# A 64-byte gap ahead of GT's tile and a 40-column offset inside wk's slot, in a gated mix of a long convolution and linear attention

## The chip, the core and the metric

The kernel runs on one core of one Trainium2 chip. The metric is the device time of one execution in microseconds (us), lower is better; 1 us is 1000 ns. TensorE (PE) does the matmuls and, beside them, loads the weights of the next one (PEld); DVE is VectorE, ACT is ScalarE, POOL is GpSimd, SP issues the DMAs.

## What is computed

Input x has 2048 rows of 640 columns. The result mixes two branches with a gate per row:

```python
g = _sigmoid((x * gate_w).sum(-1, keepdims=True))
a = _A_ref(x, ...)       # per column: convolution with a kernel of length 2048, plus x * Dskip
b = _B_ref(x, wqkv, wo)  # linear attention: 32 heads of 20 columns
return g * a + (1 - g) * b
# in _B_ref: phi(t) = where(t > 0, t + 1, exp(t)) + 1e-6
#   kv = sum_s phi(k)_s v_s ; z = sum_s phi(k)_s
#   o  = phi(q) kv / (phi(q) z + 1e-6) ; b = o @ wo
```

## The kernel before

Every fp32 matrix is held as two float32r tiles, a high part `h` (a rounded copy) and a low part `l` (the rest), and a product is three matmuls, all accumulated in one PSUM bank. This is `mm3` (line 104): high by high, low by high, high by low. In a matmul one operand is loaded into the array beforehand (128 columns, the stationary one, PEld's `LDWEIGHTS`), the other streams past it (the moving one, up to 512 columns). `pe.matmul(out, a, b)` has `a` stationary and `b` moving. In rows of the profile, `fp<-pTh,Mh` names the moving tile first and the stationary one second.

The work has three stretches.

1. **Start, to about 36 us.** The first four row tiles of x and the weights wk arrive by DMA, are split into high and low, and the key products of those four tiles are computed as the pieces land (`k_first`, line 441; matmuls at L449).
2. **The loop over T = 1 to 15 (line 530), to about 147 us.** Each round computes, for the 128 rows of tile T, the keys in two halves: `k_mm(T, 0)` (line 183) multiplies by `wkA`, 320 columns of wk and two copies of the gate's column, so 322 moving columns, 15 matmuls; `k_mm(T, 1)` multiplies by `wkB`, 320 moving columns, 15 matmuls. Around these stand the matmuls of tile T-1 that sum phi(k) against x: `g_main` (L224, L225, L227; 512 moving columns) in the blocks 0, then 1 and 2, then 3 and 4, and `g_rest` (L238 to L240; 320 moving columns). The order of one round on TensorE from T = 4 on is k_mm by wkA (15), g block 0 (3), g blocks 1 and 2 (6), k_mm by wkB (15), g_rest (6), g blocks 3 and 4 (6). Meanwhile ACT and DVE apply phi and split the next tiles, DVE runs the scan of the convolution, and SP moves x, wv and the convolution's y.
3. **The plan (line 63, run from line 728), to the end.** `q_block` (line 630) computes a 128 by 512 tile of the queries in 15 matmuls of 512 columns, with a slice of wq stationary and x transposed moving; there are 20 of them. `kv_mm` and `m_mm` fold kv and wo into a 640 by 640 matrix M, which goes to DRAM and comes back in two tiles, `Mh` and `Ml` (`m_load`, line 692). `final_mm` (line 705) computes a 128 by 512 tile of the output in 15 matmuls with a slice of M stationary and `pqT` (phi of q, normed) moving; there are 20, the last one in two halves of 256 columns. DVE adds y to each and SP stores it.

Tiles of the pool `pc` stand in SBUF one behind the other in the order in which the program names their tags, at a fixed place for the whole run. A tag is a slot, and later tiles of the same tag take it over: slot `m1` holds GT and later Mh, `m2` holds Wv and later Ml, `wAh` and `wAl` hold `wkA` and later `wqA` (the first three of wq's five column blocks), `wBh` and `wBl` hold `wkB` and later `wqB`. The slot of `wA` has rows of 384 columns, since wqA needs them; wkA uses 322 of these. The pools `pk`, `pw` and `pq` (x, phi(k), y, the raw weights and others) come behind `pc`. The pool `px`, with x transposed (`xTh`, `xTl`) and later `pTh`, `pTl` in the same slots, stands ahead of it.

Of the kernel before, what the change touches and what calls it, by code (L numbers as in the profile page):

```python
# [39 lines left out]
P = 128  # L40
# [7 lines left out]
CA, CB = 320, 320  # L48
# [9 lines left out]
NK = sum(map(len, CONV_K.values()))  # L58
WQ = 3, 4, 0, 1, 2
QI = DH // NB  # L60


PLAN = """
# [10 lines left out]
def f32(ap):  # L74
    return ap.bitcast(F32)


def body(tc, i, outT):
    nc = tc.nc
    pe, act, dve, pool, sp = nc.tensor, nc.scalar, nc.vector, nc.gpsimd, nc.sync  # L80
# [17 lines left out]
    def hi(dst, src):  # L98
        act.activation(dst, src, AF.Copy)  # L99
# [9 lines left out]
    def col(tag, n=NB, dt=F32):  # L109
        return pc.tile([P, n], dt, tag=tag, name=tag)  # L110

    def w_tiles(n, tag, name):
        return tuple(pc.tile([P, NB, n], F32R, tag=tag + x, name=name + x) for x in "hl")
# [30 lines left out]
    zc, zs, ch = col("zc"), col("zs", 1), col("ch", 1)  # L144
    zsh, zsl = col("zsh", 2, F32R), col("zsl", 2, F32R)
    bm, zh = col("bm", P, F32R), col("zh", H)
    GT = pc.tile([P, NB, D], F32, tag="m1", name="GT")
    Wv = pc.tile([P, NB, D], F32, tag="m2", name="Wv")
    M_d = [dram.tile([D, D], F32, name=f"M_d{x}") for x in "hl"]
# [55 lines left out]
    def k_split(t):  # L205
# [4 lines left out]
        dve.scalar_tensor_tensor(l, e, EPS, f32(h), op0=OP.add, op1=OP.subtract)  # L210
        za = zacc.rearrange("p (b h i) -> p b h i", h=H, i=QI)
        dve.tensor_tensor(za, za, e.rearrange("p (h b i) -> p b h i", b=NB, i=QI), op=OP.add)
        ks[t] = (h, l)
# [28 lines left out]
    def g_out(b, eng):  # L242
        src = gps.pop(b)
        (hi if eng is act else dve.tensor_copy)(GT[:, b, :512], src)

# [4 lines left out]
    def parts(gi):  # L250
        c0, n = GRP[gi]
        return [(r, c0 + o, min(HC, n - o)) for r, o in ((0, 0), (64, HC)) if o < n]
# [13 lines left out]
    def kv_mm(pr):  # L266
        p = pqp.tile([P, 512], F32, tag="f", bufs=3, name="kvps")
        kvT = kvs[pr] = kvz[pr % 2]
        for k, gi in enumerate((2 * pr, 2 * pr + 1)):
            for b in range(NB):  # L270
                for r, c, n in parts(gi):
                    pe.matmul(p[r : r + n, k * 64 : k * 64 + n], Wv[:, b, c : c + n], GT[:, b, c : c + n],
                              start=(b == 0), stop=(b == NB - 1))
# [175 lines left out]
                pe.matmul(kp[t, hf][:, :n], (xTl if ps == 1 else xTh)[0][:, b, sl], w[ps // 2][:, b, :n],  # L449
                          start=b + ps == 0, stop=b == NB - 1 and ps == 2)  # L450

    wkA = w_tiles(3 * P, "wA", "wkA")
    wkB = w_tiles(CB, "wB", "wkB")
    raw = {}

# [59 lines left out]
    def wq_views(w, c, b0, b1):  # L515
        src = raw[c][:, :D].rearrange("p (h b i) -> p b h i", b=NB, i=QI)[:, b0:b1]
        return [src] + [v[:, c, : (b1 - b0) * P].rearrange("p (b h i) -> p b h i", h=H, i=QI) for v in w]

# [11 lines left out]
    for T in range(1, NT):  # L530
# [45 lines left out]
        if T == 2:  # L576
            act.activation(dtc, dtc, AF.Exp)
            dve.tensor_reduce(zh, ident.rearrange("p (h i) -> p h i", i=QI), axis=AX.X, op=OP.add)
            dve.tensor_copy(bm.rearrange("p (h i) -> p h i", i=QI), zh[:, :, None].to_broadcast([P, H, QI]))
        for b in CONV_P.get(T - 1, ()):  # L580
# [39 lines left out]
    def rem_out():  # L620
        for b0, b1 in ((0, 4), (4, NB)):
            tp = mbank("tp")
            for b in range(b0, b1):
                pe.transpose(tp[:, (b - b0) * P : (b - b0 + 1) * P], rem[:, b * P : b * P + P], ident)
            hi(GT[:, b0:b1, 512:], tp[:, : (b1 - b0) * P].rearrange("p (b s) -> p b s", s=P))

# [314 lines left out]
```

## Time and profile before

| | |
|---|---|
| median of 3 runs | 303.79 us (303.33 to 304.34) |
| profiled execution, its time | 304.36 us |
| profiled execution, its span | 302.6 us |
| granted TensorE clock | 0.999 |
| PE busy | 296.6 us, 98% of the span, 1627 matmuls |
| PEld busy | 255.7 us, 85% |
| DVE busy | 230.0 us, 76% |
| ACT busy | 118.8 us, 39% |
| POOL busy | 46.9 us, 15% |

The span runs from the first instruction to the last; the execution's time has 1.8 us around it. In the rows of the timeline the first number is the start in us and the second the length of the row. The lengths of matmuls overlap: one begins long before the one ahead of it is written out. What a matmul costs is therefore the distance from its start to the start of the next, which I call its spacing, and not its length.

### The profile page before, as it was taken

How to read it: one execution, taken by the hardware profiler on the slowest of the kernel's cores; microseconds unless marked ns; L12 is line 12 of the kernel's file. 1: busy time of each engine (PE TensorE's matmuls, PEld its weight loads, DVE VectorE, ACT ScalarE, POOL GpSimd, SP SyncE). 2: the span in 40 equal slices, each digit the busy share in tenths (PEclk: the TensorE clock that was granted, in tenths of full speed). 3: DMA queues.
4: the chain of work that ended last, by engine and by line, in shares of the span. 5: the costliest groups of instructions: out<-in, count | busy, mean ns of one | idle time of the engine just before them, and what ended most of it. 6: DMA issues, size and time to landing. Idle time of an engine off the chain costs nothing.

```text
span 302.6 us, 4538 instructions
## 1 busy us (share of the span) xinstructions
PE 296.6 (98%) x1627; PEld 255.7 (85%) x1627; DVE 230.0 (76%) x356; ACT 118.8 (39%) x249; POOL 46.9 (15%) x50
## 2 busy tenths in 40 slices
PE   8999999999999999999999999999999999999994
PEld 8998899999999999998887767888888888788884
DVE  2859976899899799946636779859684767788992
ACT  4465143453444435317343563651423234303200
POOL 3605240000000000000000000003133211242531
PEclk9999999999999999999999999999999999999999
DMA  6827275167868756290344553790415022244323
GB/s 190 302 88 220 77 233 185 36 192 203 256 150 252 225 181 203 80 281 14 100 147 137 205 176 110 259 341 9 114 59 186 25 77 62 69 141 172 122 92 109
DMA packets 28410, 46.00 MB, mean 152 GB/s; under 512 B 3772, under 2 KB 10828, under 8 KB 28384
## 3 DMA queue, kind: packets, MB, share of 16 engines
q1 hardware_dynamic: 28383, 45.66, 48.2%
q8 instruction: 15, 0.25, 0.4%
q14 instruction: 12, 0.09, 0.1%
HBM read 32.92 MB, written 12.72 MB: 151 GB/s over the span
## 4 chain that ended last, share of the span: by engine, by line
PE 87%; DVE 6%; DMA 3%; issue 1%; ACT 1%; SPq 1%; POOL 0%; DVEq 0%; ACTq 0%; POOLq 0%
PE fp L105 8%; PE fp L107 8%; PE fp L106 8%; PE qp L105 6%; PE qp L107 6%; PE qp L106 6%; PE k L107 6%; PE k L106 6%; PE k L105 6%; PE g L227 5%; PE g L224 5%; PE g L225 5%; PE g L449 4%; DMA M_dl<-Mgl 2%; PE r L240 1%; PE r L239 1%
## 5 line engine op out<-in xcount | busy, mean ns | idle before, releaser
L434 POOL TENSOR_TENSOR yb<-yb,gb 128x512 f32<-128x512 f32 x20 | 29.5, 1482 | 220.5 <-DMA yb<-y_d 199.2
L105 PE MATMUL fp<-pTh,Mh 128*128 128x512 f32 (+1 forms) x105 | 40.1, 382 | 0.6 <-DVE o L720 0.6
L107 PE MATMUL fp<-pTl,Mh 128*128 128x512 f32 (+1 forms) x105 | 40.2, 383 | 0.0
L106 PE MATMUL fp<-pTh,Ml 128*128 128x512 f32 (+1 forms) x105 | 40.0, 381 | 0.0
L645 DVE SCALAR_TENSOR_TENSOR qe<-qe,qr 128x512 f32<-128x512 f32 x20 | 14.1, 704 | 23.8 <-ACT qr L642 23.8
L224 PE MATMUL g<-ph,xh 128*128 128x512 f32 x80 | 31.6, 395 | 0.0
L225 PE MATMUL g<-ph,xl 128*128 128x512 f32 x80 | 31.5, 394 | 0.0
L199 ACT ACTIVATE e<-k 128x320 f32<-128x320 f32 x25 | 11.0, 439 | 51.3 <-PE k L107 51.3
L99 ACT ACTIVATE pTh<-qe 128x512 fp32r<-128x512 f32 x20 | 12.6, 633 | 40.5 <-DVE qe L681 40.4
L203 DVE SCALAR_TENSOR_TENSOR e<-e,r 128x320 f32<-128x320 f32 x32 | 16.0, 504 | 14.0 <-ACT r L200 13.9
L227 PE MATMUL g<-pl,xh 128*128 128x512 f32 x80 | 26.4, 395 | 0.1
L105 PE MATMUL qp<-xTh,wqAh 128*128 128x512 f32 x60 | 24.0, 401 | 0.0
L641 ACT ACTIVATE qe<-qp 128x512 f32<-128x512 f32 x20 | 12.0, 598 | 30.6 <-PE qp L107 26.6
L105 PEld LDWEIGHTS fp<-pTh,Mh 128*128 128x128 f32 x105 | 19.7, 188 | 5.0 <-DVE o L720 1.0
L107 PE MATMUL qp<-xTl,wqAh 128*128 128x512 f32 x60 | 23.7, 394 | 0.0
L106 PE MATMUL qp<-xTh,wqAl 128*128 128x512 f32 x60 | 23.6, 393 | 0.0
L106 PEld LDWEIGHTS fp<-pTh,Ml 128*128 128x128 f32 x105 | 19.7, 188 | 4.1
L107 PEld LDWEIGHTS fp<-pTl,Mh 128*128 128x128 f32 x105 | 19.8, 188 | 3.9
L414 DVE TENSOR_TENSOR_SCAN y<-y,cY,zero 128x512 f32<-128x512 f32 x16 | 20.5, 1278 | 0.8 <-ACT y L413 0.8
L102 DVE TENSOR_TENSOR pTl<-qe,pTh 128x512 fp32r<-128x512 f32 x20 | 15.1, 763 | 6.8 <-ACT pTh L99 6.3
L107 PE MATMUL k<-wkAl,xTh 128*128 128x322 f32 x60 | 19.0, 317 | 0.0
L106 PE MATMUL k<-wkAh,xTl 128*128 128x322 f32 x60 | 18.9, 315 | 0.0
(168 smaller groups left out, 718.2 us busy)
## 6 DMA issues: line engine op xcount, KB each, us to landing
xraw<-in_x SPq DMA_DIRECT2D x16, 320.0 KB, 5.0
u<-in_xT SPq DMA_DIRECT2D x20, 256.0 KB, 5.3
out_T<-o SPq DMA_DIRECT2D x19, 256.0 KB, 2.5
y_d<-y SPq DMA_DIRECT2D x16, 256.0 KB, 2.2
yb<-y_d SPq DMA_DIRECT2D x16, 256.0 KB, 3.1
xTraw<-in_xTt SPq DMA_DIRECT2D x12, 320.0 KB, 4.5
Wv<-in_wv SPq DMA_DIRECT2D x5, 320.0 KB, 6.8
Mh<-M_dh SPq DMA_DIRECT2D x5, 320.0 KB, 4.6
```

Source lines behind the costliest of these rows:

```text
L99: act.activation(dst, src, AF.Copy)
L102: (eng or dve).tensor_tensor(dst, src, f32(h), op=OP.subtract)
L105: pe.matmul(out, ah, bh, start=start, stop=False)
L106: pe.matmul(out, al, bh, start=False, stop=False)
L107: pe.matmul(out, ah, bl, start=False, stop=stop)
L203: dve.scalar_tensor_tensor(e, e, 1.0, r[:, :n], op0=OP.min, op1=OP.add)
L224: pe.matmul(gps[b], xh[:, s], h[:, :512], start=t == 0, stop=False)
L225: pe.matmul(gps[b], xl[:, s], h[:, :512], start=False, stop=False)
L227: pe.matmul(gps[b], xh[:, b * P : b * P + P], l[:, :512], start=False, stop=t == NT - 1)
L414: dve.tensor_tensor_scan(y, y, zero.to_broadcast([P, 512]), cY[:, c], op0=OP.add, op1=OP.add)
L434: pool.tensor_tensor(ys[j], ys[j], gbs[j // NB], op=OP.mult)
L645: dve.scalar_tensor_tensor(e, e, 1.0, r, op0=OP.min, op1=OP.add)
```

## The change

Two edits. A tile `gap` of 16 fp32 columns, 64 bytes in each partition, is named just ahead of GT and set to zero on POOL. And `wkA` becomes a view into its slot that begins at column 40 of each row of 384, so that its 322 columns stand in columns 40 to 361; writers and readers go through the same view.

```diff
+WKO = 40
...
     bm, zh = col("bm", P, F32R), col("zh", H)
+    gap = col("gap", 16)
+    pool.memset(gap, 0.0)
     GT = pc.tile([P, NB, D], F32, tag="m1", name="GT")
...
-    wkA = w_tiles(3 * P, "wA", "wkA")
+    wkA = tuple(v[:, :, WKO : WKO + CA + 2] for v in w_tiles(3 * P, "wA", "wkA"))
```

No instruction is moved on PE, DVE, ACT or SP, and none changes its shape or its waits. POOL has one more. These are its rows at the start, up to the first piece of wk's low part, before:

```order
L121 MEMSET ones 128x128
L132 MEMSET zacc 128x640
L135 MEMSET cY 128x5
L135 MEMSET zero 128x1
L141 MEMSET kvT_100 128x128
L141 MEMSET kvT_101 128x128
L102 ISA
L102 TENSOR_TENSOR wkAl<-wraw,wkAh 128x322 x5
```

And the same place now, where the lines have moved by 1 to 3:

```order
L122 MEMSET ones 128x128
L133 MEMSET zacc 128x640
L136 MEMSET cY 128x5
L136 MEMSET zero 128x1
L142 MEMSET kvT_100 128x128
L142 MEMSET kvT_101 128x128
L149 MEMSET gap 128x16
L103 ISA
L103 TENSOR_TENSOR wkAl<-wraw,wkAh 128x322 x5
```

One memset stands ahead of the first `wkAl`. Everything else that changes is where tiles lie. The table gives, from the layout of the two programs, the place of each matmul's operands within their partition, as the remainder of the byte address by 512. The slices of a stationary operand step by 512 bytes, rows of the transposed x and of pT by 2048, of M by 2560, of wkA and wqA by 1536, of wkB and wqB by 1280 (so these alternate between two remainders). The last two columns are moving minus stationary.

| matmuls | stationary, before -> after | moving, before -> after | difference before | after |
|---|---|---|---|---|
| `fp` (final_mm) | M: 64 -> 128 | pT: 128 | +64 | 0 |
| `qp`, blocks 0 to 2 | wqA: 64 -> 128 | xT: 128 | +64 | 0 |
| `qp`, blocks 3 and 4 | wqB: 64, 320 -> 128, 384 | xT: 128 | +64, -192 | 0, 256 |
| `k` by wkA | xT: 128 | wkA: 64 -> 288 | -64 | +160 |
| `k` by wkB | xT: 128 | wkB: 64, 320 -> 128, 384 | -64, +192 | 0, 256 |
| `g` (g_main) | x: 320 -> 384 | phi(k): 320 -> 384 | 0 | 0 |
| `r` (g_rest) | phi(k): 320 -> 384 | x: 320, 64 -> 384, 128 | 0, 256 | 0, 256 |

## The prediction

> **What bounds the kernel now.** I read the page's busy times and chain first, then the busy times by stretch, then the timeline of PE in pieces of half a microsecond. The page says what sets the end:
>
> ```profile
> PE 296.6 (98%) x1627; PEld 255.7 (85%) x1627; DVE 230.0 (76%) x356; ACT 118.8 (39%) x249; POOL 46.9 (15%) x50
> PE 87%; DVE 6%; DMA 3%; issue 1%; ACT 1%; SPq 1%; POOL 0%; DVEq 0%; ACTq 0%; POOLq 0%
> ```
>
> PE is busy for 98% of the span, and 87% of the chain that ended last is PE. In the busy times by stretch (start and end, length, then PE, PEld, DVE, ACT and POOL) PE has no hole in the loop or in the first part of the plan:
>
> ```profile
> 36.00:142.00 106.00, 106.00 (x615) 98.04 (x614) 88.38 (x148) 46.60 (x107) 3.71 (x6) 1.00 0.60 180
> 182.00:235.00 53.00, 53.00 (x229) 42.90 (x228) 39.71 (x53) 20.76 (x37) 9.88 (x7) 1.00 0.49 157
> 264.00:299.00 35.00, 34.58 (x165) 28.82 (x165) 30.05 (x33) 6.53 (x11) 13.79 (x9) 1.00 0.38 130
> ```
>
> The granted clock is 1.00 in all three. DVE, the next engine, has 88.38 of 106.00 us, 39.71 of 53.00 and 30.05 of 35.00: it could follow a PE that is faster by one or two per cent. So the change is worth what it does to the spacing of matmuls, nothing else. A busy PE is not an even one. Two pieces of the plan run the same shape at different spacings:
>
> ```profile
> 203.50 0.40 PE L105 MATMUL fp<-pTh,Mh 128*128 128x512 f32 x1
> 203.73 0.40 PE L106 MATMUL fp<-pTh,Ml 128*128 128x512 f32 x1
> ...
> 235.00 0.39 PE L666 MATMUL dp<-acch,bm 128*128 128x512 f32 x1
> 238.90 0.39 PE L105 MATMUL qp<-xTh,wqAh 128*128 128x512 f32 x1
> 239.14 0.39 PE L106 MATMUL qp<-xTh,wqAl 128*128 128x512 f32 x1
> 239.36 0.39 PE L107 MATMUL qp<-xTl,wqAh 128*128 128x512 f32 x1
> 239.59 0.39 PE L105 MATMUL qp<-xTh,wqAh 128*128 128x512 f32 x1
> ...
> 256.07 0.39 PE L105 MATMUL fp<-pTh,Mh 128*128 128x512 f32 x1
> ```
>
> From 203.50 to 235.00 stand nine tiles, fp and qp in turn, of 15 matmuls: 31.50 us, 3.50 a tile, 233.3 ns a matmul. From 238.90 to 256.07 stand five tiles: 17.17 us, 3.434 a tile, 228.9 ns. The work, the clock and the operands' places are the same in both; two rhythms exist, and which one holds depends on how the stretch was entered. A third, shorter one stands in the g matmuls at the end of the loop:
>
> ```profile
> 143.01 0.39 PE L225 MATMUL g<-ph,xl 128*128 128x512 f32 x1
> 143.23 0.39 PE L224 MATMUL g<-ph,xh 128*128 128x512 f32 x1
> 143.46 0.39 PE L225 MATMUL g<-ph,xl 128*128 128x512 f32 x1
> 143.69 0.84 PE L227 MATMUL g<-pl,xh 128*128 128x512 f32 x3
> 144.37 0.30 PE L238 MATMUL r<-xh,ph 128*128 128x320 f32 x1
> ```
>
> Six matmuls of 512 columns in 1.36 us, 226.7 ns each: the shortest steady spacing of this width that I find, so I call it the floor. The keys by wkA, 322 columns, have two rhythms as well. These are the first of the 15 matmuls, and the first matmul behind them, in rounds T = 4, 5, 6 and 15, and where T = 7 begins:
>
> ```profile
> 36.09 0.31 PE L105 MATMUL k<-wkAh,xTh 128*128 128x322 f32 x1
> 38.30 0.40 PE L224 MATMUL g<-ph,xh 128*128 128x512 f32 x1
> 44.81 0.31 PE L105 MATMUL k<-wkAh,xTh 128*128 128x322 f32 x1
> 47.02 0.40 PE L224 MATMUL g<-ph,xh 128*128 128x512 f32 x1
> ...
> 53.77 0.31 PE L105 MATMUL k<-wkAh,xTh 128*128 128x322 f32 x1
> 56.06 0.40 PE L224 MATMUL g<-ph,xh 128*128 128x512 f32 x1
> 56.78 0.40 PE L224 MATMUL g<-ph,xh 128*128 128x512 f32 x1
> 62.63 0.31 PE L105 MATMUL k<-wkAh,xTh 128*128 128x322 f32 x1
> ...
> 133.45 0.31 PE L105 MATMUL k<-wkAh,xTh 128*128 128x322 f32 x1
> 135.74 0.40 PE L224 MATMUL g<-ph,xh 128*128 128x512 f32 x1
> ```
>
> In T = 4 the block takes 2.21 us (147 ns a matmul), in T = 6 2.29 us (153 ns); the round takes 8.72 and 8.86 us. T = 5 (44.81 to 47.02) goes like the first; T = 15 (133.45 to 135.74) goes like the second, as do the ones between. The weight loads by form, first for 36 to 51 us, then for 54 to 142 us, show who is held up (count, busy us, mean ns):
>
> ```profile
> L106 PEld LDWEIGHTS k<-wkAh,xTl 128*128 128x128 f32 x10 | 1.9, 188 | 0.1
> L106 PEld LDWEIGHTS k<-wkAh,xTl 128*128 128x128 f32 x50 | 9.6, 192 | 0.4
> ```
>
> A load beside the slow wkA stream takes 192 ns, beside the quick one 188. The two rhythms of each width differ by 6.6 and 6.7 ns. Per column, a matmul costs (226.7 - 147) / (512 - 322) = 0.42 ns, so this step is the time of 16 columns, or 64 bytes of one partition. That is my reading of the trace: the moving stream and the weight load of the next matmul meet in SBUF, one gives way by one step of 64 bytes, and whether they meet depends on their places and on the phase.
>
> **The change part by part.** The memset of `gap`. Nearest rows, POOL's timeline:
>
> ```profile
> 1.53 0.35 POOL L141 MEMSET kvT<- 128x128 f32 x2
> 4.27 0.99 POOL L102 TENSOR_TENSOR wkAl<-wraw,wkAh 128x322 fp32r<-128x322 f32 x1 [2.39 <-DVE wkAh L487]
> ```
>
> Two memsets of 128 columns took 0.35 us together, so one of 16 costs between nothing and 0.2 us, and POOL then idles 2.39 us until DVE has cast wkAh. Cost 0; without that cover it would be up to 0.2 us ahead of the first key matmuls. The writers of wkA (DVE's cast, POOL's subtraction) write the same shape with the same row step: 0.
>
> M and wq. The stationary start moves from 64 to 128 modulo 512, and the moving one stays at 128, so the difference becomes 0 (wqB: 0 or 256). That is the difference that g has now, and r has 0 and 256. The g matmuls are the nearest rows: same width, same alternation of a high and a low stationary, long enough at 143 us to be steady, and there they stand at 226.7 ns. I take the floor for M and wq. The counts, from the groups of PE by form, and behind them two rows of the timeline:
>
> ```profile
> L105 PE MATMUL fp<-pTh,Mh 128*128 128x512 f32 x95 | 37.4, 393 | 0.6 <-DVE o L720 0.6
> L105 PE MATMUL qp<-xTh,wqAh 128*128 128x512 f32 x60 | 24.0, 401 | 0.0
> L105 PE MATMUL qp<-xTh,wqBh 128*128 128x512 f32 x40 | 15.8, 395 | 0.0
> ...
> 176.33 0.40 PE L105 MATMUL qp<-xTh,wqAh 128*128 128x512 f32 x1
> ...
> 179.60 0.39 PE L107 MATMUL qp<-xTl,wqAh 128*128 128x512 f32 x1
> ```
>
> 95 + 60 + 40 = 195 groups of three, five to a tile: 39 tiles. At the floor a tile takes 15 x 0.2267 = 3.40 us. Ten tiles run at 3.50 now (the nine above, and one whose first and last start, 14 spacings apart, are 176.33 and 179.60), the other 29 near 3.434. Saving: 10 x 0.10 + 29 x 0.034 = 1.0 + 1.0 = 2.0 us. Bounds: the shorter end is 2.0; at the longer end all 39 go to 3.50, which costs 29 x 0.066 = 1.9 us. I take 2.0 saved since g is the nearest row.
>
> wkA. The difference goes from -64 to +160, half a step of 64 bytes off: no matmul in this trace has such a difference. The nearest rows are its own two rhythms. If T = 6 to 15 run like T = 4, ten blocks save 0.08 each, 0.8 us; if T = 4 and 5 run like the rest, 2 x 0.08 = 0.2 us is lost; one more step on all 180 matmuls would cost 180 x 6.7 ns = 1.2 us. I take 0.8 saved: a stationary and a moving stream half a step apart have the least cause to fall into the meeting at -64, which took hold only after two of twelve rounds.
>
> wkB, g, r. wkB goes from -64 and 192 to 0 and 256, the differences of r; both widths are 320 columns. The rows for r:
>
> ```profile
> 51.51 0.31 PE L238 MATMUL r<-xh,ph 128*128 128x320 f32 x1
> ...
> 52.38 0.39 PE L224 MATMUL g<-ph,xh 128*128 128x512 f32 x1
> 49.31 0.31 PE L105 MATMUL k<-wkBh,xTh 128*128 128x320 f32 x1
> ```
>
> Six r matmuls take 0.87 us (145 ns), 15 by wkB from 49.31 to 51.51 take 2.20 us (147 ns): the same within rounding, cost 0. The g and r operands move together. But g behind a slow wkA block is slow too: the three from 56.06 to 56.78 us stand 0.24 us apart. Round T = 6 is 0.14 us longer than T = 4, and the wkA block explains 0.08; the other 0.06 over ten rounds is 0.6 us, which I keep for the range.
>
> Sum against the profiled execution: 304.36 - 2.0 - 0.8 = 301.6 us. This execution lies 0.6 us above the median, so 303.79 - 2.8 = **301.0 us** on the scale of the median.
>
> The Trainium skill (SBUF — State Buffer, section "Who interferes with whom") gives PE two independent read ports, one for the moving operand and one for the weight load, and says that PE never waits on anyone. By that rule the shift would save nothing, and the sum would stay at 303.8 us. The rows above speak against it: one shape at 147 and 153 ns with a load of 188 and 192 ns. No run here yet shows places alone doing it.
>
> **The rivals.**
>
> *Nothing moves (0.25).* The rhythm is set by how a stretch is entered, whatever the places: 203 and 239 us show both rhythms at the same places. Then the sum is 303.8 us, or 303.0 with wkA's 0.8 alone. A measurement of this kernel tells about 0.3%, 0.9 us, from no change, so both fall under the same. Against it: in this trace 226.7 ns stands over six matmuls only where the difference is 0.
>
> *M and wq gain, wkA stays (0.20).* 303.8 - 2.0 = 301.8 us.
>
> *Slower (0.20).* With stationary and moving tiles at the same place modulo 512, load and stream meet every time, and the long rhythm, now in 10 tiles of 39, takes all of them: 29 x 0.066 = 1.9 us, 305.7 us; with wkA one step worse 306.9. For it: the g matmuls at 56.06 us have the difference 0 and stand at 240 ns. Against it: they come right behind a slow block, and the longer run at 143 us came down to the floor. It decides from the point at which more than about half of the tiles, 29 x 0.066 / 2 = 1 us, lock in the long rhythm.
>
> **How the numbers follow.** Forecast 0.35, M and wq alone 0.20, nothing 0.25, slower 0.20. Faster by over 0.3%: 0.55; within: 0.25; slower: 0.20. The likeliest case alone spans 300.2 (with the 0.6 of g and 0.2 of scatter) to 301.8. For 8 in 10 the range takes in the second and third case and part of the slower one, whose price holds only if all tiles lock: 300.2 to 305.2 us.
>
> **What would show it.** Right: tiles of fp and qp 3.40 us long, with starts 0.227 apart, through 182 to 296 us; rounds of the loop near 8.72 us from T = 6 on; wkA's loads at 188 ns; PE still 98% busy. Half right: 3.40 with rounds still at 8.86. Wrong: tiles at 3.43 and 3.50 in other places than now (entry decides, not place), or 3.50 throughout. If PE's spacing falls and the time does not, PE will show idle time behind DVE at L720, where one wait of 0.6 us stands now.

## The result and the profile after

| | before | changed |
|---|---|---|
| median of 6 runs | 304.06 us (303.33 to 305.27) | 301.80 us (301.31 to 302.20) |
| ratio to before, 95% interval | | 0.9913 [0.9898, 0.9928] |
| span of the profiled execution | 302.6 us | 300.0 us |

The changed kernel is faster: by the ratio 0.87%, which is 2.6 us of 304.06, by the two medians 2.3 us. (Before was measured again beside it, so its median has moved from 303.79.) The profiled execution of the changed kernel took 301.86 us. Its page, busy times and chain:

```profile
PE 294.0 (98%) x1627; PEld 255.3 (85%) x1627; DVE 230.7 (77%) x356; ACT 118.4 (39%) x249; POOL 46.5 (15%) x51
PE 89%; DVE 5%; issue 1%; ACT 1%; DMA 1%; SPq 1%; POOL 0%; DVEq 0%; ACTq 0%; POOLq 0%
```

PE is busy 2.6 us less over the same 1627 matmuls, and still 98% of a span that is 2.6 us shorter. Lines are now 1 to 3 higher, so L105 to L107 of `mm3` are L106 to L108. The timeline of the stretch of nine fp and qp tiles that took 31.50 us:

```profile
202.07 0.39 PE L106 MATMUL fp<-pTh,Mh 128*128 128x512 f32 x1
...
205.50 0.39 PE L106 MATMUL qp<-xTh,wqBh 128*128 128x512 f32 x1
...
232.70 0.40 PE L669 MATMUL dp<-acch,bm 128*128 128x512 f32 x1
```

The first tile takes 3.43 us, since the way in from dp still costs something; the eight behind it take 27.20 us, 3.40 each, 226.7 ns a matmul. That is the floor named in the prediction, and the long stretches of tiles from 184 us on all come down to it. Tiles between other work, most of them before 184 us, do not: they take 3.49 to 3.59. Round T = 6 of the loop, the block by wkA and the start of round 7:

```profile
54.05 0.31 PE L106 MATMUL k<-wkAh,xTh 128*128 128x322 f32 x1
56.27 0.39 PE L227 MATMUL g<-ph,xh 128*128 128x512 f32 x1
62.78 0.31 PE L106 MATMUL k<-wkAh,xTh 128*128 128x322 f32 x1
```

2.21 us for the block (2.29 before; the rows, rounded, give 2.22) and 8.73 for the round (8.86). The weight loads of that stretch, 54 to 142 us:

```profile
L107 PEld LDWEIGHTS k<-wkAh,xTl 128*128 128x128 f32 x50 | 9.4, 188 | 0.4
```

They last 188 ns, no longer 192. The new memset on POOL, and what follows it:

```profile
1.81 0.11 POOL L149 MEMSET gap<- 128x16 f32 x1
4.40 0.98 POOL L103 TENSOR_TENSOR wkAl<-wraw,wkAh 128x322 fp32r<-128x322 f32 x1 [2.48 <-DVE wkAh L490]
```

0.11 us, and POOL still idles 2.48 us behind it. One place became slower, the last tile with its two halves of 256 columns. Before, from the timeline:

```profile
295.49 0.28 PE L105 MATMUL fp<-pTh,Mh 128*128 128x256 f32 x1
295.83 0.28 PE L105 MATMUL fp<-pTh,Mh 128*128 128x256 f32 x1
```

And changed:

```profile
295.26 0.28 PE L106 MATMUL fp<-pTh,Mh 128*128 128x256 f32 x1
...
295.62 0.28 PE L106 MATMUL fp<-pTh,Mh 128*128 128x256 f32 x1
```

Three matmuls took 0.34 us and take 0.36, so the 30 of this tile cost 0.2 us more. How much of that is the place is open: the kernel with everything moved alike (below), which has the differences of before, took 1.77 us for the first 15 of them, against 1.70 before and 1.79 now.

Where the time went, from the starts in the two timelines: up to round 4, 36.09 us before and 36.35 now (+0.26; in the other kernels below this start lies anywhere from 35.8 to 36.8 us, so it says nothing of the change); rounds 4 to 15, up to the first `zp` matmul behind the loop, 110.54 and 109.34 (-1.20); from there to the first fp, 56.87 and 56.38 (-0.49; this piece took 56.51 in the kernel with the memset alone, where no tile moves, so part of it is scatter); to the last dp, 59.68 and 58.56 (-1.12); to the last matmul, 35.26 and 35.24 (-0.02). Together -2.57, the difference of the spans.

### The profile page after: what moved, and what is told of

Its sections match the earlier page's. It is cut to its first block, busy times and chain, and to the rows that moved or that the text cites. A ratio compares the mean times of both kernels' runs of the same rounds, so it can differ in the third digit from the quotient of the medians.

```text
span 300.0 us, 4539 instructions
## 1 busy us (share of the span) xinstructions
PE 294.0 (98%) x1627; PEld 255.3 (85%) x1627; DVE 230.7 (77%) x356; ACT 118.4 (39%) x249; POOL 46.5 (15%) x51
## 4 chain that ended last, share of the span: by engine, by line
PE 89%; DVE 5%; issue 1%; ACT 1%; DMA 1%; SPq 1%; POOL 0%; DVEq 0%; ACTq 0%; POOLq 0%
PE fp L106 8%; PE fp L107 8%; PE fp L108 8%; PE qp L106 7%; PE qp L108 6%; PE qp L107 6%; PE k L107 6%; PE k L106 6%; PE k L108 6%; PE g L230 5%; PE g L228 5%; PE g L227 5%; PE g L452 4%; PE r L243 1%; PE r L242 1%
## 5 line engine op out<-in xcount | busy, mean ns | idle before, releaser
L106 PE MATMUL fp<-pTh,Mh 128*128 128x512 f32 (+1 forms) x105 | 39.9, 380 | 0.6 <-DVE o L723 0.6
L108 PE MATMUL fp<-pTl,Mh 128*128 128x512 f32 (+1 forms) x105 | 39.8, 379 | 0.0
L107 PE MATMUL fp<-pTh,Ml 128*128 128x512 f32 (+1 forms) x105 | 39.8, 379 | 0.0
L648 DVE SCALAR_TENSOR_TENSOR qe<-qe,qr 128x512 f32<-128x512 f32 x20 | 14.8, 742 | 23.0 <-ACT qr L645 23.0
L106 PE MATMUL qp<-xTh,wqAh 128*128 128x512 f32 x60 | 23.9, 398 | 0.0
L106 PEld LDWEIGHTS fp<-pTh,Mh 128*128 128x128 f32 x105 | 19.7, 188 | 4.8 <-DVE o L723 1.1
L107 PE MATMUL qp<-xTh,wqAl 128*128 128x512 f32 x60 | 23.4, 390 | 0.0
L108 PE MATMUL qp<-xTl,wqAh 128*128 128x512 f32 x60 | 23.4, 390 | 0.0
L108 PEld LDWEIGHTS fp<-pTl,Mh 128*128 128x128 f32 x105 | 19.7, 188 | 3.8
L107 PEld LDWEIGHTS fp<-pTh,Ml 128*128 128x128 f32 x105 | 19.8, 188 | 3.7
L107 PE MATMUL k<-wkAh,xTl 128*128 128x322 f32 x60 | 18.6, 310 | 0.0
L106 PE MATMUL k<-wkAh,xTh 128*128 128x322 f32 x60 | 18.6, 309 | 0.0
```

Of the source, the lines that this page charges most:

```text
L106: pe.matmul(out, ah, bh, start=start, stop=False)
L107: pe.matmul(out, al, bh, start=False, stop=False)
L108: pe.matmul(out, ah, bl, start=False, stop=stop)
L648: dve.scalar_tensor_tensor(e, e, 1.0, r, op0=OP.min, op1=OP.add)
```

## The experiments

The two theories are those of the prediction: the spacing of matmuls follows from the difference between the moving and the stationary place, or from something else (the place of one tile alone, the way into a stretch, nothing). Each timed kernel ran against the kernel before on the same chip: the first four against a median of 304.58 us, the last three against one of 304.66. The rows come from one profiled execution of each.

### The gap alone

```diff
-WKO = 40
+WKO = 0
```

> The gap alone, wkA at column 0 of its slot, so that its difference (moving minus stationary place) is 0 instead of +160. Theory 1, the difference sets the rhythm: fp and qp tiles stay at 3.40 us as in the changed kernel, wkA with the difference of r runs at 147 ns a matmul, rounds 8.73 us, time as the changed kernel, 301.8 us. Theory 2, wkA needs the half step of its own: wkA at 153 ns, rounds 8.85 us, about 1.2 us slower than the changed kernel, 303.0 us.

Measured: 301.94 us, ratio 0.9913 [0.9892, 0.9933], the same as with both edits. The timeline of one round, and of the nine tiles:

```profile
62.36 0.31 PE L106 MATMUL k<-wkAh,xTh 128*128 128x322 f32 x1
...
64.58 0.40 PE L227 MATMUL g<-ph,xh 128*128 128x512 f32 x1
...
71.11 0.31 PE L106 MATMUL k<-wkAh,xTh 128*128 128x322 f32 x1
...
201.53 0.39 PE L106 MATMUL fp<-pTh,Mh 128*128 128x512 f32 x1
...
232.16 0.40 PE L669 MATMUL dp<-acch,bm 128*128 128x512 f32 x1
```

The block by wkA takes 2.22 us, 148 ns a matmul, the round 8.75. The nine tiles take 30.63 us, as in the changed kernel (202.07 to 232.70). Theory 2 falls: wkA needs no offset of its own to leave the slow rhythm. Between this kernel and the changed one the loop differs by 0.18 us (109.52 and 109.34), which the times can't tell.

### The 40 columns alone

```diff
-    gap = col("gap", 16)
-    pool.memset(gap, 0.0)
```

> The 40 columns alone, no gap: M, wq and wkB as before, wkA's difference +96. Theory 1: fp and qp tiles at 3.43 and 3.50 us as before, wkA at 147 ns and rounds of 8.73 us, time 1.2 us under before. Rival, the stationary tile's own place decides and not the difference: xT has not moved, so nothing changes, rounds 8.85 us, time as before.

Measured: 303.63 us, ratio 0.9976 [0.9958, 0.9994], 0.7 us faster than before instead of 1.2. The timeline of one round, and of the nine tiles:

```profile
62.45 0.31 PE L106 MATMUL k<-wkAh,xTh 128*128 128x322 f32 x1
...
64.69 0.39 PE L225 MATMUL g<-ph,xh 128*128 128x512 f32 x1
...
71.21 0.31 PE L106 MATMUL k<-wkAh,xTh 128*128 128x322 f32 x1
...
202.22 0.40 PE L106 MATMUL fp<-pTh,Mh 128*128 128x512 f32 x1
...
233.13 0.39 PE L667 MATMUL dp<-acch,bm 128*128 128x512 f32 x1
```

Moving wkA alone, with the stationary tile where it was, takes the block from 2.29 to 2.24 us and the round from 8.86 to 8.76: the stationary place alone does not decide. 149 ns, not 147, so the difference +96 is worse than +160 or 0. The nine tiles take 30.91 us, 3.43 each, where before they took 31.50, though M, wq, xT and pT stand where they stood: at the difference +64 something besides the places, the way into the stretch as I read it, chooses between the two rhythms. The profiled execution, 302.93 us, was the fastest of this kernel's twelve, so that all of them run these tiles at 3.43 is not shown.

### Everything moved alike

```diff
+    gap = px.tile([P, 16], F32, tag="gap", name="gap")
     ones = col("ones", P)
...
+    pool.memset(gap, 0.0)
     GT = pc.tile([P, NB, D], F32, tag="m1", name="GT")
```

> A gap of 64 bytes at the head of everything, ahead of x transposed as well, wkA at column 0: M, wq, wkB stand where the changed kernel has them, but all differences are those of before. Theory 1, difference: as before, tiles at 3.43 and 3.50 us, rounds 8.85 us, same time as before. Rival, alignment of a tile by itself (M and wq at 128 modulo 512): tiles at 3.40 us, about 2.0 us faster than before.

Measured: 304.98 us, ratio 1.0005 [0.9989, 1.0021]. The timeline at the same places:

```profile
63.35 0.31 PE L105 MATMUL k<-wkAh,xTh 128*128 128x322 f32 x1
...
65.64 0.40 PE L226 MATMUL g<-ph,xh 128*128 128x512 f32 x1
...
72.21 0.31 PE L105 MATMUL k<-wkAh,xTh 128*128 128x322 f32 x1
...
204.00 0.40 PE L105 MATMUL fp<-pTh,Mh 128*128 128x512 f32 x1
...
235.51 0.39 PE L668 MATMUL dp<-acch,bm 128*128 128x512 f32 x1
```

M, wq and all of `pc` stand where the gap alone puts them, and the gain is gone: 2.29, 8.86 and 31.50 us, the numbers of before. All that sets this kernel apart from the gap alone is that xT and pT moved along. This settles it for the difference against the place of M and wq by themselves.

By the rule that the prediction cited from the Trainium skill (SBUF — State Buffer, section "Who interferes with whom"), that PE never waits on anyone, read as the prediction read it, these two kernels should take the same time. 0.9913 and 1.0005 say otherwise: places matter. Whether PE waits there, and for what, no run shows.

### The memset alone

```diff
+    pool.memset(zh[:, :16], 0.0)
     GT = pc.tile([P, NB, D], F32, tag="m1", name="GT")
```

> The kernel before with one more POOL memset of 16 columns at the same place in the order, into a tile that is written later anyway; no tile moves. Theory 1: same time and same rhythms as before. Rival, the extra instruction shifts the entry into the stretches: other tiles at 3.40 or 3.50 us than before, time anywhere from 2 us faster to 2 us slower.

Measured: 304.32 us, ratio 0.9990 [0.9973, 1.0007]. The nine tiles by the timeline:

```profile
203.67 0.40 PE L105 MATMUL fp<-pTh,Mh 128*128 128x512 f32 x1
...
235.17 0.39 PE L667 MATMUL dp<-acch,bm 128*128 128x512 f32 x1
```

31.50 us again, and no change in the time that the interval can tell: the extra instruction alone doesn't make the gain.

### A sweep of the difference

```diff
+    for n, k in ((512, 24), (322, 24), (320, 24), (256, 24)):
+        for d in DIFF:
+            mp = pqp.tile([P, 512], F32, tag="f", bufs=3, name="sw")
+            mv = pqT[3][0].rearrange("p b s -> p (b s)")
+            for r in range(k):
+                pe.matmul(mp[:, :n], m["hl"[r % 2]][:, 0, :P], mv[:, d : d + n], start=True, stop=True)
```

> The changed kernel with 1344 more matmuls behind its last ones, which leave the output alone: for 512, 322, 320 and 256 moving columns, 24 matmuls in a row with Mh's and Ml's first 128 columns stationary in turn and a slice of pTh moving that begins 0, 2, 4, 8, 12, 16, 24, 32, 40, 48, 64, 80, 128 or 256 columns into it (difference 0 to 1024 bytes). Theory 1, meeting of load and stream in steps of 64 bytes: 512 columns at 226.7 ns for differences 0 and multiples of 256 bytes, 229 or 233 ns at 64 bytes (16 columns), 322 columns at 147 or 153 ns; the half step (8, 24, 40 columns) like its better neighbour. Rival, the difference does not matter and only the order of the three matmuls and the entry do: the same spacing at every difference of one width.

For each place the 12th and the 24th matmul give the steady spacing. The timeline for 512 columns at 0 bytes (the first two rows), 64 (the next two) and 256, then for 256 columns at 0 and at 192 bytes:

```profile
297.93 0.39 PE L780 MATMUL sw<-pTh,Ml 128*128 128x512 f32 x1
...
300.65 0.39 PE L780 MATMUL sw<-pTh,Ml 128*128 128x512 f32 x1
...
325.75 0.39 PE L780 MATMUL sw<-pTh,Ml 128*128 128x512 f32 x1
...
328.50 0.39 PE L780 MATMUL sw<-pTh,Ml 128*128 128x512 f32 x1
...
353.68 0.39 PE L780 MATMUL sw<-pTh,Ml 128*128 128x512 f32 x1
...
356.40 0.39 PE L780 MATMUL sw<-pTh,Ml 128*128 128x512 f32 x1
...
473.29 0.28 PE L780 MATMUL sw<-pTh,Ml 128*128 128x256 f32 x1
...
474.73 0.28 PE L780 MATMUL sw<-pTh,Ml 128*128 128x256 f32 x1
...
498.81 0.28 PE L780 MATMUL sw<-pTh,Ml 128*128 128x256 f32 x1
...
500.17 0.28 PE L780 MATMUL sw<-pTh,Ml 128*128 128x256 f32 x1
```

Twelve spacings in 2.72, 2.75 and 2.72 us, and in 1.44 and 1.36 us. The table gives all of them (ns, the mean of the last twelve spacings; one execution):

| difference, bytes | 512 columns | 322 | 320 | 256 |
|---|---|---|---|---|
| 0, 256, 512, 1024 | 226.7 | 148.3 | 146.7 | 120.0 |
| 8 | 233.3 | 146.7 | 146.7 | 120.0 |
| 16 | 231.7 | 147.8 | 145.3 | 116.7 |
| 32 | 233.3 | 148.9 | 146.7 | 116.7 |
| 48 | 233.3 | 146.7 | 146.7 | 118.3 |
| 64, 320 | 228.9 | 148.3 | 146.7 | 117.8 |
| 96 | 233.3 | 148.9 | 146.7 | 120.0 |
| 128 | 233.3 | 146.7 | 146.7 | 118.4 |
| 160 | 233.8 | 146.7 | 146.7 | 117.5 |
| 192 | 233.3 | 146.7 | 146.5 | 113.3 |

The rival, one spacing for each width, falls. The difference counts modulo 256: 0, 256, 512 and 1024 agree to 0.1 ns, as do 64 and 320. At 512 columns 0 is the one good place of this list, and +64, where M and wq stood, is the second. At 322 columns 0 is not the best; 160, where the changed kernel has wkA, is at 146.7, and the gap alone at 148.3, as measured in its loop. 192, the place of wkA before (-64), stands at 146.7 here, so the 153 ns that the loop showed is a rhythm that this way in did not find. At 256 columns 0 is among the worst, 120.0 ns against 117.8 at +64; before, the last tile ran at 113.3, quicker than the sweep shows for its place, so the place explains a part of its loss only. The half step is no good neighbour at 32 and 96 bytes; that part of the expectation missed.

### Which two operands meet

```diff
+    for d in (16, 24, 32, 48):
+        for cross in (0, 1):
...
+            for r in range(48):
+                s, v = (r % 2) * d, ((r + cross) % 2) * d
+                pe.matmul(mp, m["hl"[r % 2]][:, 0, s : s + P], mv[:, v : v + 512], start=True, stop=True)
```

> The changed kernel with 384 more matmuls of 512 columns behind its last ones, which leave the output alone. Two stationary places, s and s + D, and two moving places, v and v + D (s and v at the same place modulo 256), taken in turn, 48 matmuls for each of D = 64, 96, 128, 192 bytes and for each of two pairings. Straight: s with v, then s + D with v + D; each matmul's own difference is 0, and the weights that are loaded during a stream differ from it by D. Crossed: s with v + D, then s + D with v; the own difference is D, and the weights that are loaded during a stream stand at its place. Theory 1, the load of the next weights meets the stream that runs: crossed at 226.7 ns, straight at 229 to 233 ns. Rival, a matmul's own pair decides: straight at 226.7 ns, crossed at 229 to 233 ns.

Measured, mean of the last 24 spacings, straight and crossed: D = 64, 231.7 and 231.7 ns; 96, 234.3 and 230.0; 128, 236.7 and 230.0; 192, 231.7 and 233.3. The timeline for 128 bytes, twelve spacings each, straight and then crossed:

```profile
348.51 0.40 PE L780 MATMUL sw<-pTh,Ml 128*128 128x512 f32 x1
...
351.35 0.40 PE L780 MATMUL sw<-pTh,Ml 128*128 128x512 f32 x1
...
359.63 0.39 PE L780 MATMUL sw<-pTh,Ml 128*128 128x512 f32 x1
...
362.39 0.39 PE L780 MATMUL sw<-pTh,Ml 128*128 128x512 f32 x1
```

2.84 and 2.76 us. Neither pairing comes down to 226.7 at any D, so the number that theory 1 gave for crossed and the one that the rival gave for straight both missed. At 96 and 128 bytes the crossed one is shorter by 4 to 7 ns, the direction of theory 1; at 64 they are equal, at 192 it is longer. Which two operands meet stays open.

### A finer sweep

```diff
+    DIFF = (1, 3, 5, 6, 10, 14, 18, 20, 28, 36, 44, 52, 56, 58, 60, 62)
+    for n, k in ((512, 24), (322, 24), (320, 24)):
```

> The sweep of differences again at 16 more places (1, 3, 5, 6, 10, 14, 18, 20, 28, 36, 44, 52, 56, 58, 60, 62 columns) for 512, 322 and 320 moving columns, 24 matmuls each, behind the changed kernel's last ones. Theory 1: no place goes under 226.7 ns at 512 columns, most stand at 233.3; at 322 and 320 columns 146.7 to 149 ns, 145.3 near a difference of 16 bytes. Rival, the place 0 is only one good place among many: some of the new ones run under 226.7 or 145 ns, and a better layout than the changed one exists.

Measured: at 512 columns 228.9 to 236.7 ns, nothing under 226.7. At 322 columns 144.4 at 24 bytes, 146.7 to 150.0 elsewhere. At 320 columns 146.7 to 153.3, so the 145.3 at 16 bytes stays the lowest. So the rival holds at 322 columns and falls at 512: in the sweeps there are better places for wkA and wkB, for M and wq none among the 26 tried (modulo 256).

### One side at a time

```diff
+    for d in (4, 8, 16, 32):
+        for st2, mv2, base in ((d, 0, 0), (0, d, 0), (0, 0, d)):
...
+                s, v = base + (r % 2) * st2, base + (r % 2) * mv2
```

> The changed kernel with 432 more matmuls of 512 columns behind its last ones, 36 in a row of each kind, for D = 16, 32, 64 and 128 bytes. Kind 1: the stationary place alternates between difference 0 and D, the moving place is fixed. Kind 2: the moving place alternates, the stationary is fixed. Kind 3: both stand still at D, difference 0. Theory 1, the difference alone: kind 3 at 226.7 ns for every D, kinds 1 and 2 at 228 to 237 ns. Rival, the moving tile's own place modulo 256 counts, whatever is loaded: kind 3 is longer than 226.7 ns, kind 1 stays near 226.7.

Measured, mean of the last twelve spacings, kinds 1, 2 and 3: D = 16, 230.0, 231.7, 230.0 ns; 32, 235.0, 230.0, 226.7; 64, 232.3, 231.9, 226.7; 128, 232.2, 230.0, 226.7. The timeline of kind 3 at 64 and at 128 bytes, twelve spacings each:

```profile
367.88 0.39 PE L780 MATMUL sw<-pTh,Ml 128*128 128x512 f32 x1
...
370.60 0.39 PE L780 MATMUL sw<-pTh,Ml 128*128 128x512 f32 x1
...
392.73 0.39 PE L780 MATMUL sw<-pTh,Ml 128*128 128x512 f32 x1
...
395.45 0.39 PE L780 MATMUL sw<-pTh,Ml 128*128 128x512 f32 x1
```

2.72 us both. Moved together by 32, 64 or 128 bytes the pair keeps the floor; moved together by 16 bytes it does not. So for shifts of 32, 64 and 128 bytes the difference alone counts, and at 16 the place counts too; theory 1 missed there. With either side alternating, the floor is gone.

### Better places for wkA and wkB

```diff
-WKO = 40
+WKO = 6
```

> The changed kernel with wkA 6 columns into its slot instead of 40, so that its difference is 24 bytes, where the fine sweep showed 144.4 ns at 322 columns against 146.7 at the changed kernel's 160. If the steady spacing of the sweep carries over into blocks of 15 matmuls, 180 x 2.3 ns = 0.4 us faster than the changed kernel, 301.4 us. Rival, a block of 15 is mostly the way into the rhythm and not the rhythm: no gain, 301.8 us or up to 0.5 us slower.

```diff
+    def wb_tiles(off, name):
+        return tuple(pc.tile([P, NB * CB + 64], F32R, tag="wB" + x, name=name + x)[:, off : off + NB * CB]
+                     .rearrange("p (b n) -> p b n", b=NB) for x in "hl")
...
-    wkB = w_tiles(CB, "wB", "wkB")
+    wkB = wb_tiles(4, "wkB")
...
-            wqB = w_tiles(CB, "wB", "wqB")
+            wqB = wb_tiles(0, "wqB")
```

> As the one before, and wkB 4 columns (16 bytes) into a slot that is 64 columns longer; wq keeps its difference of 0. The sweep had 145.3 ns at 320 columns and 16 bytes against 146.7 at 0. If steady spacings carry over, another 180 x 1.4 ns = 0.25 us, 301.1 us. Rival: as for the one before, no gain.

And the changed kernel once more, for the comparison:

> The changed kernel itself once more, to stand beside the two others on the same chip. Every theory expects the ratio of 0.991 to the kernel before.

Measured: 301.81 us, 0.9916 [0.9897, 0.9935], with wkA at 24 bytes; 301.55 us, 0.9905 [0.9886, 0.9924], with wkB at 16 as well; 302.43 us, 0.9930 [0.9912, 0.9948], for the changed kernel itself. The timeline of the kernel with both, block by wkA, g, block by wkB, next round:

```profile
53.44 0.31 PE L106 MATMUL k<-wkAh,xTh 128*128 128x322 f32 x1
...
55.62 0.39 PE L231 MATMUL g<-ph,xh 128*128 128x512 f32 x1
...
57.70 0.31 PE L106 MATMUL k<-wkBh,xTh 128*128 128x320 f32 x1
...
62.15 0.31 PE L106 MATMUL k<-wkAh,xTh 128*128 128x322 f32 x1
```

The block by wkA takes 2.18 us instead of 2.21, but the nine g behind it 2.08 instead of 2.06: more than half of the gain is given back on the way into the next width. The round is 8.71 us against 8.73, the whole loop 109.04 against 109.34 (109.20 with wkA alone at 24 bytes, a gain of 0.14 where 0.4 was expected). The steady spacings do carry over into the block; the 0.3 us that is left is inside the intervals, so this kernel beats the kernel before, and is not shown to beat the changed one. In its second profiled execution the changed kernel has its rhythms again: rounds of 8.73 us, the loop 109.34.

## Why the prediction was right, point by point

**PE alone bounds it, so spacing is the term.** Right. DVE, ACT and DMAs kept up, the spans fell by what the spacings gave, and the wait for DVE's `o` grew only from 0.56 to 0.64 us.

**M and wq go to the floor.** Right in mechanism: 3.40 us a tile, 226.7 ns, in every stretch long enough to settle, and undone by moving xT and pT along. The size was 2.0 us; the 39 tiles, from the start of each to the start of what follows, saved 1.8, and from the end of the loop to the last matmul it was 0.49 + 1.12 + 0.02 = 1.6. Two things were not priced. A stretch needs some matmuls to find the rhythm (eight spacings behind dp, whose two matmuls are the first, up to ten in the sweep), and the first fp tile still takes 3.43. The prediction counted 29 tiles near 3.434, but eight of these stand between other work: they took 3.53 to 3.63 before, 3.49 to 3.59 after, and gained little. And the 30 matmuls of 256 columns lost 0.2 us: I carried what g shows at 512 columns over to all of M's matmuls, and the sweep shows that the good place depends on the width.

**wkA.** Predicted 0.8 us with 0.6 more left in the range for g; the loop gave 1.2. The block itself gave the 0.8 (2.29 to 2.21 us in ten rounds), and the nine g behind it, 2.10 us before and 2.06 now, the other 0.4. The reason was wrong. I argued that a place half a step off has the least cause to meet. The gap alone, which puts wkA at 0, ends the slow rhythm as well, and the sweep has the half steps at 32 and 96 bytes among the worse ones. Of the two edits the gap makes the gain; with the gap in, the 40 columns are worth 0.18 us in the loop and nothing that the times can tell.

**The sum.** It is in part luck. 2.0 and 0.8 were predicted, 1.6 and 1.2 measured: both make 2.8, since one miss undoes the other. Part of the gain in M and wq, 0.6 us in the nine tiles, hangs on the slow rhythm in which they ran before, and in the profiled execution with the 40 columns alone that was gone as well, without moving M or wq.

**The reading behind it.** Predicted: the weight load of the next matmul meets the running stream, and one gives way by 64 bytes. That spacing follows the difference of the two places is shown (the gap alone against everything moved alike, and the sweep). That it is the next load and the running stream is not: the pairing did not separate it, and with either side alternating the floor was lost. Nor is the step of 64 bytes: it would give 226.7 and 233.3 ns at 512 columns, and the sweeps have values all the way from 228.9 to 236.7. What exactly collides stays open.

**The rivals.** "Nothing moves" falls for the difference 0, but its core, that the way in chooses the rhythm, holds at +64: the nine tiles took 31.50 us before and 30.91 with the 40 columns alone, M, wq, xT and pT at the same places. "M and wq gain, wkA stays" named 301.8 us, the very median that was measured, while the ratio turns 303.79 into 301.1, next to the forecast of 301.0. The time alone doesn't decide between the two; the rival falls by the trace: rounds at 8.73 us, not 8.86. "Slower" did not occur at 512 columns, and did, on a small scale, at 256.

## What to carry to other kernels

When PE is the bound and its matmuls are of one shape, compare the spacing of starts in several stretches of the timeline; two values for one shape mean that something besides the work sets them. Here the distance between the stationary and the moving tile, modulo 256 bytes, was worth 0.9% for 64 bytes of padding. The good distance has to be measured for each width, in long runs and in the block lengths of the kernel, since it took up to ten matmuls here to find a rhythm.

## What the runs showed of the hardware that was not expected

- At 512 float32r columns 226.7 ns was reached only at a difference of 0 modulo 256 bytes; the 25 other places tried in the sweeps stood between 228.9 and 236.7 ns, up to 4.4% longer, at a granted clock of 1.00.
- Two rhythms can be stable at one difference: 228.9 and 233.3 ns at +64 with 512 columns, 147 and 153 ns at -64 with 322, 113.3 and 117.8 ns at +64 with 256.
- A common shift of both operands by 16 bytes cost 3.3 ns a matmul (230.0 against 226.7), shifts of 32, 64 and 128 bytes nothing.
- 322 columns can run at 144.4 ns, below the 146.7 of 320 columns at most places.
